# Attention with mixed heads: seven high parts move to ScalarE, and each part of v is split two slots ahead of its products

## The chip, the cores and the metric

The kernel runs on one core of one Trainium2 chip. The metric is device time in microseconds (us) of one execution. In this text TensorE is PE in the rows, VectorE is DVE, ScalarE is ACT, GpSimd is POOL, and SyncE, whose queue issues most DMAs, is SP.

## The reference

Four batches, twelve heads, 448 positions, 64 columns a head. Scores of all heads are mixed with `w_pre` ahead of the softmax and with `w_post` behind it; two gated layers follow.

```python
scores = scale * np.matmul(q, k.transpose(0, 1, 3, 2))
scores = np.einsum('bhij,hg->bgij', scores, w_pre)
scores = scores - np.max(scores, axis=-1, keepdims=True)
attn = np.exp(scores)
attn = attn / (np.sum(attn, axis=-1, keepdims=True) + 1e-09)
attn = np.einsum('bhij,hg->bgij', attn, w_post)
out = np.matmul(attn, v)
...
h = (x @ w1) * (x @ w2) @ w3
x = h @ w_out
out = np.maximum(x @ w_in, 0.0) ** 2 @ w_out2
```

## The kernel before

Products that need more than 16 bits are made of two parts: a high part (rounded) and a low part (what is left), and three products of parts.

The 448 rows of a batch are cut into four pieces of 110, 110, 110 and 118 rows (`SUP`, numbered s = 0 to 15; piece 4b is the first of batch b), and each piece into blocks of ten rows (`BLK`, numbered u = 0 to 179, the last of a batch of eight rows). A main loop goes over slots, one per block, and writes out by hand the order of all engines. In slot u stand, among others:

- the DMA of block u + 5 from the scores (`regroup`, `Bt<-S`, L279), at the slot's end, on SP's queue;
- in odd slots, the mixing product of blocks u + 1 and u + 2 (`premix`, L285, TensorE), which reads `Bt`; one premix is two matmul records, so a pair is four;
- the negated row maximum (`negmax`, L299, VectorE) and the exponential (`expo`, L307, ScalarE) of block u;
- of block u - 2 the high part `EH` (`split_h`), made by GpSimd (L354), or, for odd blocks from `LAST_EH` = 166 on, by ScalarE (L352); of odd blocks GpSimd makes the low part too (L365, L366), of even blocks VectorE makes it one slot later (L368);
- the second mixing product of block u - 4 (`postmix`, L381, TensorE) and the eviction of block u - 5 in two parts, `ATh` by ScalarE (L397) and `ATl` by VectorE (L403). The product has two PSUM buffers, so a postmix waits for `ATl` of two blocks earlier;
- what a table of events adds: `qk` (scores of a later piece) and `av` (products with v of an earlier piece, L495) at the end of a slot; `split_k`, `split_kl` (L197, GpSimd), `split_q`, `split_ql` (L227), `split_v` (the high part `Vh`, L467, ScalarE) and `split_vl` (the low part `Vl`, L474, VectorE), the last four behind the slot's other work; the evictions of `av` (`put_xh`, `put_xl`, L523) and their stores (`store_x`, L531, SP).

Each batch's v comes in six parts (two heads each), and piece 4b needs them first. Its two raw buffers (`vraw`) are used again for the first two chunks of the later layers' weights, which SP's queue loads in slots 153 and 156:

```python
v_last = first[NSUP - 4]
W_LOADS = (v_last + 18, v_last + 21)
...
        if u in W_LOADS:
            load_to(W_LOADS.index(u) + 1)
```

`first[s]` is the first block of piece s; `v_last` is 135. These loads stand at the start of their slots. A load into a buffer waits for the last reader of what was in it, and SP's queue issues in order. k of batch b is split in six steps, one in every second slot: blocks 26 to 36 for batch 1, 70 to 80 for batch 2, 116 to 126 for batch 3.

Of the kernel before, what the change touches and what calls it, by code (L numbers as in the profile page):

```python
# [35 lines left out]
def talking_heads_attention_moe_moe2(  # L36
# [28 lines left out]
    SUP = []  # L65
# [199 lines left out]
    NB = len(BLK)  # L265
# [73 lines left out]
    def inverse(u):  # L339
        return nsum[u][: BLK[u][2] * H, 5, u % 2 : u % 2 + 1]  # L340

    def seven(x):
        return x.rearrange("p (a b) -> p a b", a=EG)

    def low_on_pool(u):
        return u % 2 == 1

    def split_h(u):
        n = BLK[u][2] * H
        EH[u] = bp.tile([NBK, S], F16, tag="EH", name="EH", bufs=4)  # L350
        if low_on_pool(u) and u >= LAST_EH:
            nc.scalar.activation(seven(EH[u][:n]), Ex[u][:n], AF.Copy, scale=inverse(u))  # L352
            return
        nc.gpsimd.tensor_scalar(  # L354
            seven(EH[u][:n]), Ex[u][:n], inverse(u), 1.0, op0=ALU.mult, op1=ALU.mult
        )
# [47 lines left out]
            ATs[s][1][:, :, :, a], src, ATs[s][0][:, :, :, a], op=ALU.subtract  # L404
        )

    LAST_EH = NB - 14

    def v_raw():
        return bp.tile([P, 6 * NCH, D], F32, tag="vraw", name="vraw", bufs=2)  # L410
# [129 lines left out]
    first = {}  # L540
# [7 lines left out]
    LOAD, FIRST, MID, LOW, END = range(5)  # L548

    def at(slot, kind, f, *a):  # L550
        events.setdefault(slot, []).append((kind, len(events), f, a))

    low_k = set()
    for s in range(2, NSUP):
        b = SUP[s][0]
        base = first[s - 1]
        L = first[s] - base
        qs = [base - 4 + p * L // NDC for p in range(NDC)]
        for p in range(NDC):
            at(qs[p], END, qk, s, p)  # L560
            at(qs[p] + 1, FIRST, evict_s, s, p)
            if p % 3 == 0:
                at(qs[p] - 9, LOAD, load_q, s, p // 3)
                at(qs[p] - 5, MID, split_q, s, p // 3, None)
                at(qs[p] - 4 + (p == 0 and qs[p] - 4 in low_k), LOW, split_ql, s, p // 3)
        if s % 4 == 0:
            ks = [(first[s - 2] + 4) // 2 * 2 + 2 * p for p in range(NDC)]
            for p in range(NDC):
                assert ks[p] + 1 < qs[p]
                at(ks[p], MID, split_k, b, p, None)  # L570
                at(ks[p] + 1, LOW, split_kl, b, p)
                low_k.add(ks[p] + 1)
                at(ks[p] - 4, LOAD, load_k, b, p)
    for b in range(B):
        f = first[4 * b]
        for i, slot in ((0, 9), (2, 11), (4, 13)):
            at(f + slot, MID, scale_v, b, i)
        for hg in range(2):
            for i in range(3):
                if b or hg:  # L580
                    at(f - 4 + 3 * hg + i if b else i + 1, LOAD, load_v, b, hg, i)
                at(f + 3 * hg + i + 1, MID, sum_v, b, hg, i)
                at(f + 3 * hg + i + 13, MID, split_v, b, hg, i)
                at(f + 3 * hg + i + 14, LOW, split_vl, b, hg, i)
    qk_at = sorted(x for x in events if any(e[2] is qk for e in events[x]))
    for s in range(NSUP - 1):
        for p in range(NDC):
            lo = first[s + 1] + LAG + 1
            at_qk = [x for x in qk_at if lo <= x < lo + SUP[s + 1][3]]
            slot = at_qk[p] if len(at_qk) == NDC else lo + (0, 1, 3, 4, 6, 7)[p]  # L590
            for part in range(2):
                at(slot, END, av, s, p, part)
            if p % 3 == 2:
                at(slot + 1, FIRST, put_xh, s, p // 3)
                at(slot + 1, MID, put_xl, s, p // 3)
                if s < NSUP - 2:
                    at(slot + 2, END, store_x, s, p // 3)
# [511 lines left out]
    for u in range(NB + LAG + 2):  # L1109
# [38 lines left out]
        if 0 <= u - 2 < NB:  # L1148
            split_h(u - 2)
            if low_on_pool(u - 2):  # L1150
                split_l(u - 2)
# [459 lines left out]
```

## Time and profile before

| what | value |
|---|---|
| time, median of 3 runs | 1283.51 us (1282.63 to 1283.73) |
| the profiled execution: its time, its span | 1283.09 us, 1281.4 us |
| TensorE, busy share of the span | 98% |
| VectorE, ScalarE, GpSimd, busy share | 76%, 55%, 34% |
| attention part (180 slots) | about the first 440 us |

The span runs from the first to the last instruction; the time has 1.7 us around it. Once the start is over, a pair of slots takes between 4.1 and 6.0 us (from one `expo` of an even slot to the next).

### The profile page before, as it was taken

What the parts mean: (1) busy time and instruction counts of PE and PEld (TensorE: products, weight loads), DVE (VectorE), ACT (ScalarE), POOL (GpSimd) and SP (SyncE); (2) the same over time, 40 slices, a digit from 0 to 9 for tenths busy, and PEclk for the clock granted to TensorE, in tenths of its full rate; (3) what the DMA queues carried; (4) which work ended last, traced back from release to release, by engine and by line L of the source; (5) the groups of instructions that cost most, each with busy time, mean ns of one, the idle gap of its engine ahead of it and who ended that gap; (6) DMA issues with size and microseconds to landing.
All of it is one profiled execution on the core that took longest, in us unless ns stands there. A gap on an engine that the chain in (4) does not pass through costs nothing. (4 is left out here: it accounts for less than half of the span.)

```text
span 1281.4 us, 25951 instructions
## 1 busy us (share of the span) xinstructions
PE 1258.4 (98%) x10192; PEld 775.3 (61%) x10192; DVE 980.1 (76%) x2032; ACT 704.1 (55%) x1367; POOL 430.9 (34%) x502
## 2 busy tenths in 40 slices
PE   7999999999999999999999999999999999999998
PEld 3666766766766655555569855555555555555555
DVE  6988897898899868876849766437568779797776
ACT  6877876877887635443424444336844353534520
POOL 3898799789878401110003200000000000001000
PEclk9999999999999999999999999999999999999999
DMA  6466455555656734354223234004141322324004
GB/s 192 122 163 166 119 149 145 151 134 139 167 147 168 212 76 110 101 109 129 91 83 132 82 79 81 9 3 87 38 107 35 90 78 38 78 49 105 5 10 173
DMA packets 82174, 132.92 MB, mean 104 GB/s; under 512 B 30820, under 2 KB 67812, under 8 KB 82052
## 3 DMA queue, kind: packets, MB, share of 16 engines
q1 hardware_dynamic: 75924, 123.45, 35.6%
q0 software_dynamic: 2992, 5.42, 3.0%
q10 hardware_dynamic: 3136, 2.40, 0.7%
q8 instruction: 80, 1.31, 0.4%
q14 instruction: 42, 0.34, 0.1%
HBM read 80.78 MB, written 11.92 MB: 72 GB/s over the span
## 5 line engine op out<-in xcount | busy, mean ns | idle before, releaser
L1046 PE MATMUL mm<-x,w 128*128 128x448 f16 x2196 | 416.7, 352 | 0.0
L1046 PEld LDWEIGHTS <-w 128*128 128x128 f16 x2304 | 224.9, 98 | 209.2
L1488 PE MATMUL mm<-w,g 128*128 128x384 f16 x1344 | 219.7, 326 | 0.0
L1488 PEld LDWEIGHTS <-g 128*128 128x128 f16 x1344 | 131.5, 98 | 87.4 <-issue 0.2
L285 PE MATMUL p<-Bt,wpre_k 120*120 120x448 f32 x360 | 158.9, 560 | 5.0 <-DMA Bt<-S 3.3
L381 PEld LDWEIGHTS <-EH 120*112 120x112 f16 (+1 forms) x1440 | 125.0, 130 | 50.9 <-issue 41.6
L354 POOL TENSOR_SCALAR EH<-E,st 120x448 f16<-120x448 f32 x173 | 127.9, 749 | 46.3 <-DVE st L337 32.2
L403 DVE TENSOR_TENSOR ATl<-o,ATh 112x480 f16<-112x480 f32 x180 | 116.2, 645 | 31.9 <-ACT ATh L397 31.7
L397 ACT CAST ATh<-o 112x480 f16<-112x480 f32 x180 | 100.9, 561 | 58.5 <-PE o L381 53.7
L381 PE MATMUL o<-wph,EH 120*112 120x120 f16 x720 | 124.1, 219 | 7.7 <-DVE ATl L403 6.4
L307 ACT ACTIVATE E<-p,st 120x448 f32<-120x448 f32 x180 | 115.7, 643 | 21.9 <-DVE st L299 12.3
L1497 DVE SCALAR_TENSOR_TENSOR acc<-mm,sv,acc 128x384 f32<-128x384 f32 x196 | 112.1, 609 | 14.2 <-PE mm L1488 13.5
L381 PE MATMUL o<-wph,EL 120*112 120x120 f16 x720 | 122.2, 216 | 0.0
L381 PE MATMUL o<-wpl,EH 120*112 120x120 f16 x720 | 122.2, 216 | 0.0
L805 POOL DMA_DIRECT2D across<-tot x23 | 12.8, 556 | 316.7 <-ACT xa L791 316.7
L299 DVE TENSOR_REDUCE st<-p 120x1 f32<-120x448 f32 x180 | 110.1, 612 | 1.7 <-PE p L285 1.5
L1046 PE MATMUL mm<-h,M 128*128 128x448 f16 x576 | 109.8, 353 | 0.7 <-ACT M L1218 0.5
L366 POOL TENSOR_TENSOR EL<-F,EH 120x448 f16<-120x448 f32 (+1 forms) x90 | 100.6, 1118 | 23.8 <-issue 16.0
L791 ACT ACTIVATE xa<-xa 128x768 f32<-128x768 f32 x54 | 45.5, 842 | 93.4 <-DVE xa L787 75.4
L381 PEld LDWEIGHTS <-EL 120*112 120x112 f16 x720 | 93.6, 130 | 0.0
L368 DVE SCALAR_TENSOR_TENSOR EL<-E,st,EH 120x448 f16<-120x448 f32 (+1 forms) x90 | 82.5, 917 | 12.7 <-POOL EH L354 11.8
L1046 PEld LDWEIGHTS <-M 128*128 128x128 f16 x576 | 55.9, 98 | 53.9 <-DVE M L1214 1.9
(217 smaller groups left out, 2057.9 us busy)
## 6 DMA issues: line engine op xcount, KB each, us to landing
Bt<-S SPq DMA_DIRECT2D x176, 210.0 KB
raw<-in_moe_w_out_dram SPq DMA_DIRECT2D x24, 768.0 KB
raw<-in_moe_w_in_dram SPq DMA_DIRECT2D x16, 768.0 KB
raw<-in_moe_w_dram SPq DMA_DIRECT2D x14, 768.0 KB
raw<-in_moe_w_dram SPq DMA_DIRECT2D x16, 512.0 KB
vraw<-in_v_dram SPq DMA_DIRECT2D x24, 224.0 KB
out_dram<-acc SPq DMA_DIRECT2D x28, 192.0 KB
kraw<-in_k_dram SPq DMA_DIRECT2D x22, 224.0 KB
```

Of the source, the lines that this page charges most:

```text
L285: nc.tensor.matmul(pt[: n * H, :S], wpre_k.rearrange("p t g -> p (t g)")[: n * H, : n * H], Bt.pop(u)[: n * H], start=True, stop=True,)
L299: nc.vector.tensor_reduce(nsum[u][:n, 0, j : j + 1], Pp[u][:n, :S], axis=AX.X, op=ALU.max, negate=True)
L307: nc.scalar.activation(e[:n], Pp.pop(u)[:n, :S].rearrange("p (a b) -> p a b", a=EG), AF.Exp, bias=t[:n, 0, j : j + 1], scale=1.0, accum_ou ...
L354: nc.gpsimd.tensor_scalar(seven(EH[u][:n]), Ex[u][:n], inverse(u), 1.0, op0=ALU.mult, op1=ALU.mult)
L366: nc.gpsimd.tensor_tensor(a, f, b, op=ALU.subtract)
L368: nc.vector.scalar_tensor_tensor(a, e, inverse(u), b, op0=ALU.mult, op1=ALU.subtract)
L381: nc.tensor.matmul(pt[:CP, c * n : (c + 1) * n], a[:n, c * CP : (c + 1) * CP], w[:n, :n], start=(i == 0), stop=(i == 2),)
L397: nc.scalar.copy(ATs[s][0][:, :, :, m * NR : m * NR + nr], src)
L403: nc.vector.tensor_tensor(ATs[s][1][:, :, :, a], src, ATs[s][0][:, :, :, a], op=ALU.subtract)
L1046: nc.tensor.matmul(pt[:, :S], w[a][:, cs], x[z][:, sl], start=(c == 0 and i == 0), stop=(c == len(parts) - 1 and i == 2),)
L1488: nc.tensor.matmul(pt[:, :OH], gs[j][a][:, ts_], ws[j][0][:, w, os_], start=(n == 0), stop=(n == 5),)
L1497: nc.vector.scalar_tensor_tensor(d, pt[:, :OH], sv[:, v : v + 1], d, op0=ALU.mult, op1=ALU.add)
```

## The change

The high part of an odd block is made by ScalarE also for the blocks in `full`. That set is filled where the first step of a batch's scores stands in an even slot, which holds for piece 8 (batch 2) alone: blocks 70 to 83, so seven odd blocks, 71 to 83. And each part of v is split at fixed distances from its own first product: `split_v` two slots ahead of `av` of piece 4b and `split_vl` one slot ahead, where before the six parts were split in six slots running, 13 to 18 slots into the batch (`split_vl` 14 to 19).

```diff
-        if low_on_pool(u) and u >= LAST_EH:
+        if low_on_pool(u) and (u in full or u >= LAST_EH):
             nc.scalar.activation(seven(EH[u][:n]), Ex[u][:n], AF.Copy, scale=inverse(u))
             return
...
-    LAST_EH = NB - 14
+    LAST_EH, full = NB - 14, set()
...
             ks = [(first[s - 2] + 4) // 2 * 2 + 2 * p for p in range(NDC)]
+            if qs[0] % 2 == 0:
+                full.update(range(ks[0], ks[-1] + 4))
...
                 at(f + 3 * hg + i + 1, MID, sum_v, b, hg, i)
-                at(f + 3 * hg + i + 13, MID, split_v, b, hg, i)
-                at(f + 3 * hg + i + 14, LOW, split_vl, b, hg, i)
...
             slot = at_qk[p] if len(at_qk) == NDC else lo + (0, 1, 3, 4, 6, 7)[p]
+            if s % 4 == 0:
+                b = SUP[s][0]
+                assert slot - 2 > first[s] + 13
+                at(slot - 2, MID, split_v, b, *divmod(p, 3))
+                at(slot - 1, LOW, split_vl, b, *divmod(p, 3))
```

For batch 3 the six low parts stood in slots 149 to 154; they stand now in slots 150, 152, 153, 155, 157 and 159. The weight loads of slots 153 and 156 stay where they were.

GpSimd's queue where k of batch 2 is split (`EH`, `F` and `EL` are the parts of a block, `kl` and `ql` low parts of k and q), a piece of the difference:

```order
-L354 TENSOR_SCALAR EH<-E,st 120x448 x2
-L365 TENSOR_SCALAR F<-E,st 120x7x64
-L366 TENSOR_TENSOR EL<-F,EH 120x448
-L197 TENSOR_TENSOR kl<-kraw,kh 128x448
...
+L354 TENSOR_SCALAR EH<-E,st 120x448
+L365 TENSOR_SCALAR F<-E,st 120x7x64
+L366 TENSOR_TENSOR EL<-F,EH 120x448
+L197 TENSOR_TENSOR kl<-kraw,kh 128x448
```

One of the two `EH` of each pair of slots is gone from there, seven in all.

VectorE's queue around the last low part of v of batch 3, before:

```order
L299 TENSOR_REDUCE st<-p 120x1
L323 TENSOR_SCALAR st<-st 120x6
L337 RECIPROCAL st<-st 120x2
L403 TENSOR_TENSOR ATl<-o,ATh 112x48x10
L474 SCALAR_TENSOR_TENSOR Vl<-vraw,vs,Vh 112x512
```

and of the change (L785 and L789 are the first steps of decoding the first weight chunk):

```order
L403 TENSOR_TENSOR ATl<-o,ATh 112x48x10
L785 TENSOR_SCALAR Vh<-vraw 128x768
L789 TENSOR_SCALAR kraw<-kraw 128x768
L299 TENSOR_REDUCE st<-p 120x1
L368 SCALAR_TENSOR_TENSOR EL<-E,st,EH 120x448
L403 TENSOR_TENSOR ATl<-o,ATh 112x48x10
L474 SCALAR_TENSOR_TENSOR Vl<-vraw,vs,Vh 112x512
```

The last low part moved from slot 154 to the end of slot 159, behind `ATl` of block 154.

SP's queue around the two weight loads (`vraw<-in_moe_w_dram`), with what each DMA waits for, before:

```order
L729 DMA vraw<-in_moe_w_dram 128x1536 [waits DMAHW1_49,DVE_49]
L279 DMA Bt<-S 120x1x448 [waits DMAHW2_49,PE_49]
L279 DMA Bt<-S 120x1x448 [waits DMAHW3_49,PE_49]
L279 DMA Bt<-S 120x1x448 [waits DMAHW4_49,PE_49]
L729 DMA vraw<-in_moe_w_dram 128x1536 [waits DMAHW5_49,DVE_49,Activation_49]
L531 DMA x_d<-xt 128x3x110 [waits DMAHW6_49,Activation_49]
L531 DMA x_d<-xt 128x3x110 [waits DMAHW7_49,DVE_49]
L279 DMA Bt<-S 120x1x448 [waits DMAHW0_49,PE_49]
```

and of the change, where the load's line is L734:

```order
L734 DMA vraw<-in_moe_w_dram 128x1536 [waits DMAHW1_49,DVE_49,Activation_49]
L279 DMA Bt<-S 120x1x448 [waits DMAHW2_49,PE_49]
L279 DMA Bt<-S 120x1x448 [waits DMAHW3_49,PE_49]
L279 DMA Bt<-S 120x1x448 [waits DMAHW4_49,PE_49]
L734 DMA vraw<-in_moe_w_dram 128x1536 [waits DMAHW5_49,DVE_49,Activation_49]
L531 DMA x_d<-xt 128x3x110 [waits DMAHW6_49]
L531 DMA x_d<-xt 128x3x110 [waits DMAHW7_49]
L279 DMA Bt<-S 120x1x448 [waits DMAHW0_49,PE_49]
```

No DMA changed its place. Behind the second load the two stores no longer wait for ScalarE and VectorE themselves: the load ahead of them waits for later instructions of both, the last `Vh` of batch 3 (slot 158) and the last `Vl` (slot 159). The first load waits for the `Vl` of slot 153. The `Bt` right behind the stores is that of block 161, whose premix stands in slot 159; the three ahead of the second load are blocks 158 to 160.

## Rows read from the trace of the kernel before

**Rows 1.** the page's first part: busy us and share of each engine

```profile
PE 1258.4 (98%) x10192; PEld 775.3 (61%) x10192; DVE 980.1 (76%) x2032; ACT 704.1 (55%) x1367; POOL 430.9 (34%) x502
```

**Rows 2.** busy us by engine, six slot pairs, k of batches 1, 2 split

```profile
80.48:108.33 27.85, 27.02 (x352) 18.75 (x351) 23.55 (x50) 20.09 (x45) 27.35 (x31) 1.00 0.57 146
187.13:217.16 30.03, 27.34 (x351) 19.10 (x348) 24.47 (x50) 19.81 (x45) 29.53 (x33) 1.00 0.49 121
```

**Rows 3.** waits of PE, 187-217, 48-56, 258-272 us: total us, times, longest

```profile
PE o L381 <- DVE ATl L403: 2.7, 4, 0.9
...
PE o L381 <- DVE ATl L403: 1.0, 1, 1.0
...
PE o L381 <- DVE ATl L403: 1.1, 2, 0.8
```

**Rows 4.** waits of DVE, 185 to 215 us

```profile
DVE EL L368 <- POOL EH L354: 4.7, 4, 1.4
```

**Rows 5.** one line's instructions, POOL's high part and ACT's: ns least/median/most

```profile
L354 POOL TENSOR_SCALAR EH<-E,st x173: 632/642/1850, 22.7 to 435.6; 120x448 f16<-120x448 f32 x170, 96x448 f16<-96x448 f32 x3
...
L352 ACT ACTIVATE EH<-E,st x7: 655/657/689, 411.2 to 441.7; 120x448 f16<-120x448 f32 x6, 96x448 f16<-96x448 f32 x1
```

**Rows 6.** VectorE's low part of v, all 24: ns least/median/most

```profile
L474 DVE SCALAR_TENSOR_TENSOR Vl<-vraw,vs,Vh x24: 733/905/1393, 48.7 to 378.6; 112x512 f16<-112x512 f32 x24
```

**Rows 7.** timeline of DVE: start us, us, line, tiles

```profile
263.54 0.51 DVE L523 SCALAR_TENSOR_TENSOR xt<-a,xt 128x354 f16<-128x354 f32 x1
```

**Rows 8.** timeline of PE, first product with Vl

```profile
265.31 0.21 PE L495 MATMUL a<-ATh,Vl 112*64 112x110 f16 x2
```

**Rows 9.** timeline of SP: when DMAs were issued

```profile
373.71 0.45 SPq L729 DMA_DIRECT2D vraw<-in_moe_w_dram  x1
...
379.53 0.47 SPq L729 DMA_DIRECT2D vraw<-in_moe_w_dram  x1
380.30 1.82 SPq L531 DMA_DIRECT2D x_d<-xt  x2
382.21 9.40 SPq L279 DMA_DIRECT2D Bt<-S  x6
```

**Rows 10.** timeline of DVE: low parts of v, and ATl of block 154

```profile
376.00 0.33 DVE L219 CAST qh<-qraw 128x354 fp32r<-128x354 f32 x1
...
378.56 0.90 DVE L474 SCALAR_TENSOR_TENSOR Vl<-vraw,vs,Vh 112x512 f16<-112x512 f32 x1
...
389.25 0.65 DVE L403 TENSOR_TENSOR ATl<-o,ATh 112x480 f16<-112x480 f32 x1
```

**Rows 11.** timeline of PE: premix of blocks 158, 159 and 160, 161

```profile
383.59 1.76 PE L285 MATMUL p<-Bt,wpre_k 120*120 120x448 f32 x4
...
388.05 1.76 PE L285 MATMUL p<-Bt,wpre_k 120*120 120x448 f32 x4
```

**Rows 12.** DMAs by kind: count, KB each

```profile
Bt<-S SPq DMA_DIRECT2D x176, 210.0 KB
...
x_d<-xt SPq DMA_DIRECT2D x44, 82.5 KB
...
vraw<-in_moe_w_dram SPq DMA_DIRECT2D x2, 768.0 KB
```

**Rows 13.** windows, last columns the granted clock, DMA share, GB/s

```profile
380.00:388.00 8.00, 8.00 (x115) 5.83 (x113) 7.33 (x16) 6.85 (x16) 7.83 (x10) 1.00 0.82 239
384.00:385.00 1.00, 1.00 (x4) 0.50 (x3) 1.00 (x2) 1.00 (x4) 1.00 (x2) 1.00 0.87 287
```

**Rows 14.** windows at the end of the span

```profile
1280.00:1281.00 1.00, 0.00 (x0) 0.00 (x0) 0.00 (x0) 0.00 (x0) 0.00 (x0) 0.85 0.00 0
```

**Rows 15.** timeline of PE at the end of the span

```profile
1273.69 3.90 PE L1488 MATMUL mm<-w,g 128*128 128x384 f16 x23
```

**Rows 16.** timeline of PE: the first filler products, and later ones

```profile
1.26 3.29 PE L622 MATMUL a<-ATl 128*128 128x512 f16 x8 [1.26 <-DVE ATl L617]
...
22.48 1.03 PE L622 MATMUL a<-ATl 128*128 128x512 f16 x4
```

## The prediction

> **What bounds the kernel now.** I read the page first: TensorE is busy for 1258.4 of 1281.4 us [rows 1], so the kernel is as long as TensorE's queue, and a change outside TensorE can only give or take the waits in it, 23.0 us in all. Then I asked for TensorE's waits in the stretches that the change touches. Where k of batch 2 is split it waits four times, 2.7 us, and in the two stretches where v of batches 0 and 2 is split once and twice, 1.0 and 1.1 us; each time a postmix needs a PSUM buffer that VectorE's `ATl` has not yet emptied [rows 3]. VectorE's own waits then say what is late ahead of that `ATl`. In the stretch of k it is GpSimd's `EH`, four times, 4.7 us [rows 4]. The windows agree: six slot pairs with the same products (352 and 351 records) take 27.85 us in batch 1 and 30.03 us in batch 2, and GpSimd is busy for 29.53 of the latter [rows 2]. Last I read SP's timeline around the two weight loads, since the order shows that their waits change.
>
> **The change, part by part.**
>
> *The seven high parts.* GpSimd loses 7 x 0.642 = 4.5 us and ScalarE gains 7 x 0.657 = 4.6 us [rows 5]. ScalarE is busy for 19.81 of the 30.03 us [rows 2], so it has 10.2 us free and takes them. GpSimd then has some 25.0 us of work in a stretch that is 27.85 us long where nothing is late, so `EH` is no longer what VectorE waits for. The gain lies between 2.2 us (30.03 less 27.85, as in batch 1, which has waits of its own) and 2.7 us (all four waits). If ScalarE were late instead it is nothing. I take 2.5.
>
> *v split later.* Where TensorE waits today, VectorE has just made low parts of v ahead of the `ATl` that is late. One costs 0.73 to 1.39 us, 0.905 in the middle [rows 6]. With the change the first of them stands behind that `ATl`, and the six are spread over ten slots instead of six. So the waits of 1.0 and 1.1 us should go; the bounds are nothing and 2.1 us, and I take 2.1, because the low parts taken away ahead of the `ATl` are as long as the waits. A new wait comes in: TensorE's first product with `Vl` now follows the low part closely. At the tightest of the 24 places VectorE is done with the instruction ahead at 264.05 us [rows 7] and the product starts at 265.31 us [rows 8], 1.26 us later. A low part of 0.905 us fits, one of 1.39 us is 0.13 us late; I take nothing, and 0.4 us (three times that) as the bound.
>
> *SP's second weight load.* Not one DMA moves, but the load of slot 156 must wait until the buffer's old content, the second half of v of batch 3, has been read, and the last reader moved to the end of slot 159. In the run before that reader ends at 378.56 + 0.90 = 379.46 us [rows 10] and the load is issued at 379.53 us [rows 9], so SP already waits for it, and everything behind stands with it. The Trainium skill says the same of any DMA: a semaphore wait happens on the issuing sequencer, the DMA engines only consume their queues ("DMA: Bandwidth & Descriptors", section "Anatomy of one DMA"); the 0.07 us between these two rows agrees, and it is the rule that speaks against this change.
>
> In the new order the reader follows `ATl` of block 154, which ends at 389.25 + 0.65 = 389.90 us [rows 10]. VectorE has by then done five low parts of the batch, as against six before, so it comes there no later. The low part ends at 390.8 us and the load is issued 11.3 us later than before. Behind it wait two stores, which nobody needs soon, and the `Bt` of blocks 161 to 164. TensorE wants block 161 in slot 159: the premixes of blocks 160 and 161 start at 388.05 us and take 1.76 us, so the second starts at 388.9 us [rows 11]. That product is held, and with TensorE's queue in order so are the postmix, `av` and all that ScalarE and VectorE would do next.
>
> How long? The load is issued in 0.47 us [rows 9], so nothing flows before 391.3 us. Then 768 + 2 x 82.5 + 210 = 1143 KB [rows 12], 1.17 MB, have to pass. In the eight busy microseconds of the run before the rate is 239 GB/s [rows 13]: 4.9 us. With 0.9 us for start and landing (my choice) block 161 is there at 397.1 us: 8.2 us of waiting. The low bound takes the best microsecond, 287 GB/s [rows 13], and no start: 4.1 us, 395.4 us, 6.5 us of waiting. The high bound is what the run before allows: there the load was issued at 379.53 us and block 161 was in place by 388.9 us, so it needed at most 9.4 us; 390.8 + 9.4 = 400.2 us, 11.3 us of waiting. I take 8.2, nearer the low end, because in the run before the stores waited too and older blocks were still in transfer. By the fit for one DMA of the Trainium skill's page "DMA: Bandwidth & Descriptors" (2.0 us plus the bytes at 436 GB/s, same section; measured on another kind of queue) the 1.17 MB would take 4.7 us, the wait would be 6.6 us and the sum 1286.6 us, an estimate.
>
> *SP's first weight load.* It now waits for the low part of slot 153, which follows the cast that ends at 376.33 us [rows 10]: 377.2 us, 3.5 us later than its 373.71 us [rows 9]. By the same reckoning (978 KB, 4.2 us) block 158 is there at 377.2 + 0.5 + 4.2 + 0.9 = 382.8 us, and TensorE wants it at 383.59 us [rows 11]. So nothing is lost, but it is near: the bound is 3.5 us, if block 158 landed just in time before. I take 0.3.
>
> *TensorE's clock.* The longest wait of rows 3 is 1.0 us; one of 8 us is new. At the end of the span the last product ends at 1273.69 + 3.90 = 1277.59 us [rows 15], and the granted clock of 1280 to 1281 us is 0.85 [rows 14], which is 1.0 (2.4 GHz) for the first 0.7 us and 0.5 (1.2 GHz) after it: it fell 3.1 us after TensorE stopped. The start shows what it takes to come back: eight filler products need 3.29 us, four later ones 1.03 us [rows 16]; the eight lost 3.29 - 2.06 = 1.2 us. I add 1.2 us, between nothing (the clock holds) and 3.3 us (all of such a stretch). The Trainium skill's rule is that the slow clock is the default state and activity lifts it ("TensorE: Matmul & The Clock Gate", "Part 1: The HAM clock gate"); rows 14 to 16 agree, and it too speaks against this change.
>
> *Sum.* Gains 2.5 + 2.1 = 4.6 us; losses 8.2 + 0.3 + 1.2 = 9.7 us; together 5.1 us longer. The attention part's delay reaches the end in full, because what follows is TensorE's queue and no later wait is that long. Against the profiled execution's 1283.09 us (0.42 us under the median, so no correction is needed): 1288.2 us.
>
> **Rivals.** *The load is not in the way* (faster). If the last `Vl` were done by 382.6 us (388.9 less the 6.3 us from issue to landing), block 161 would be in time. For it: VectorE has room where low parts were taken away. Against it: the `ATl` ahead of it reads a product of slot 158, and slot 159 starts at 388 us. Only the gains are left: 1283.1 - 4.6 = 1278.5 us. Chance 0.07.
>
> *A short wait* (about the same). The transfer runs at its best rate and the clock holds: 1283.1 - 4.6 + 6.5 = 1285.0 us. For it: the queues are empty when the load comes, unlike before. Chance 0.16.
>
> *The gains don't come* (the change doesn't do what it says). ScalarE makes `EH` ahead of the next `ATh`, so the `ATl` that GpSimd made late would be late by ScalarE, and the spread low parts, 0.9 us in slots where VectorE is busy for 23.55 of 27.85 us [rows 2], would hold back as much as before. Against it: ScalarE has 10.2 us free for 4.6. 1283.1 + 9.7 = 1292.8 us. Chance 0.10.
>
> **How the numbers follow.** My forecast, 1288.2 us, has 0.67. It and the last rival are slower by over 0.2% (2.6 us, about what a measurement of this kernel can tell): 0.77. The short wait is within 0.2%: 0.16. Faster: 0.07. The range reaches down to the short wait with somewhat more gain (4.6 + 2.5 us), 1282.5 us, and up to the high bound of the wait with 2.2 us for the clock and the first load: 1283.1 - 4.6 + 11.3 + 2.2 = 1292.0, and 1293.0 us to take in the last rival; what is left out is the first rival and the far ends. The forecast's own range is 1286 to 1292 us.
>
> **What would show it.** In the changed kernel TensorE should have one wait of 6.5 to 11.3 us in a premix, released by the DMA of `Bt`, near 385 to 395 us; SP's second weight load should be issued right after the last `Vl`, and VectorE's last `Vl` should follow the first steps of decoding. A granted clock under 1 just behind that wait shows the clock's term. The four waits of rows 3 near 200 us and those near 52, 264 and 269 us should be gone, and VectorE should no longer wait for GpSimd's `EH` there. No wait at `Bt` makes the forecast wrong by its largest term; waits of postmix near 200 us make it wrong by the gains.

## The result, and the profile after

The changed kernel takes 1292.27 us (median of 6 runs, 1290.23 to 1294.23) against 1283.68 us: 1.0065 times the time before, 95% interval 1.0052 to 1.0078. Its profiled execution took 1292.72 us, 9.63 more than the one of before. The forecast was 1288.2 us, with 1286 to 1292 us as its own range. The direction and the mechanism of the largest term were right; the time lies 0.3 us above that range, and a loss of 3.8 us was not foreseen.

The page of the changed kernel, its first line and two groups of TensorE (busy us, mean ns, then the idle time ahead of them and its releaser); the first answers to [rows 1]:

```profile
PE 1261.1 (98%) x10192; PEld 776.3 (60%) x10192; DVE 979.3 (76%) x2032; ACT 709.4 (55%) x1374; POOL 429.5 (33%) x495
...
L285 PE MATMUL p<-Bt,wpre_k 120*120 120x448 f32 x360 | 160.8, 563 | 14.6 <-DMA Bt<-S 13.7
...
L381 PE MATMUL o<-wph,EH 120*112 120x120 f16 x720 | 124.7, 219 | 5.2 <-DVE ATl L403 3.9
```

ScalarE has seven instructions more and GpSimd seven fewer, as the diff says. TensorE has 29.9 us without work in place of 23.0. Where they lie, and what else grew, is told by the lengths of stretches, worked out from the starts of the exponential (L307) of the blocks at their ends, in the profiled executions:

| blocks | what changed there | before | after | change | predicted |
|---|---|---|---|---|---|
| 0 to 10 | nothing | 19.61 | 20.13 | +0.5 | 0 |
| 10 to 24, 100 to 114 | v of batches 0, 2 split later | 31.78, 34.22 | 30.53, 32.96 | -2.5 | -2.1 |
| 24 to 40, 114 to 130 | the last low part of v stands at their start; k of batches 1, 3 is split | 36.76, 36.76 | 38.66, 38.64 | **+3.8** | 0 |
| 54 to 70, 144 to 156 | v of batches 1, 3 split later | 36.70, 28.13 | 36.31, 27.68 | -0.8 | 0 |
| 70 to 86 | seven high parts on ScalarE | 38.94 | 36.42 | -2.5 | -2.5 |
| 156 to 166 | SP's second weight load | 21.72 | 32.99 | **+11.3** | +9.7 |
| 166 to the end | | 877.28 | 877.30 | 0 | 0 |

A block stands for its slot; the stretches not listed change by 0.1 us in all. First the largest. TensorE's waits of the changed kernel from 380 to 402 us (us in total, times, longest), and SP's queue there:

```profile
PE p L285 <- DMA Bt<-S: 8.3, 2, 8.0
```

```profile
375.35 0.35 SPq L734 DMA_DIRECT2D vraw<-in_moe_w_dram  x1
...
389.47 0.35 SPq L734 DMA_DIRECT2D vraw<-in_moe_w_dram  x1
389.88 0.95 SPq L531 DMA_DIRECT2D x_d<-xt  x2
390.93 1.69 SPq L279 DMA_DIRECT2D Bt<-S  x2
```

VectorE's and TensorE's timelines give what is on either side of it:

```profile
388.66 0.75 DVE L474 SCALAR_TENSOR_TENSOR Vl<-vraw,vs,Vh 112x512 f16<-112x512 f32 x1
```

```profile
386.89 1.01 PE L285 MATMUL p<-Bt,wpre_k 120*120 120x448 f32 x2
...
395.87 1.82 PE L285 MATMUL p<-Bt,wpre_k 120*120 120x448 f32 x2 [7.96 <-DMA Bt<-S]
```

The last low part ends at 389.41 us, the load is issued 0.06 us later, the `Bt` of block 161 stands behind it and the two stores, and TensorE, out of work at 387.90 us, starts again at 395.87 us. That premix of two records takes 1.82 us where the one ahead took 1.01. The windows say why (the number ahead of the last two is the granted clock):

```profile
388.00:390.00 2.00, 0.00 (x0) 0.00 (x0) 2.00 (x5) 0.55 (x2) 1.92 (x2) 1.00 0.00 0
390.00:392.00 2.00, 0.00 (x0) 0.00 (x0) 0.17 (x2) 0.00 (x0) 0.92 (x2) 0.80 0.73 178
...
396.00:398.00 2.00, 2.00 (x8) 1.05 (x9) 0.00 (x0) 0.00 (x0) 0.00 (x0) 0.50 0.56 133
...
400.00:402.00 2.00, 2.00 (x31) 1.37 (x30) 2.00 (x4) 1.14 (x4) 1.92 (x2) 0.64 0.35 97
402.00:404.00 2.00, 2.00 (x18) 1.10 (x13) 1.89 (x6) 2.00 (x5) 1.04 (x1) 1.00 0.11 26
```

The clock falls from 1.00 (2.4 GHz) to 0.50 (1.2 GHz) while TensorE stands, about 391.2 us, and comes back near 401.4 us. So the 11.3 us are 7.96 of waiting at the second load, 0.30 at the first, and 3.0 us more, nearly all of it slow work: 5.6 us at half the speed cost 2.8 us.

Then the loss that was not predicted. TensorE's waits of the changed kernel from 86 to 108 us, where k of batch 1 is split, and where the run before waits 0.2 us for `ATl` and never for `Bt`:

```profile
PE o L381 <- DVE ATl L403: 1.3, 3, 0.7
PE p L285 <- DMA Bt<-S: 0.7, 1, 0.7
```

With a shorter wait for `E` these make 1.3 us more of waiting than before in blocks 24 to 40. The other 0.6 us of the 1.9 appears as busy time of TensorE (36.55 us in place of 35.92), whose ends are modelled.

The gains are plain. From 185 to 219 us TensorE waits once, 0.5 us, in place of four times [rows 3], and VectorE's wait for `EH` from 185 to 215 us went from 4.7 us [rows 4] to 1.8. The waits near 52, 264 and 269 us are gone.

```profile
PE o L381 <- DVE ATl L403: 0.5, 1, 0.5
```

```profile
DVE EL L368 <- POOL EH L354: 1.8, 2, 1.1
```

**Where the k split got slower.** The first two low parts of k of batch 1, with the casts of k and q (`kh`, L191; `qh`, L219) near them, on GpSimd and VectorE, before:

```profile
78.96 1.15 POOL L197 TENSOR_TENSOR kl<-kraw,kh 128x448 fp32r<-128x448 f32 x1
83.58 1.15 POOL L197 TENSOR_TENSOR kl<-kraw,kh 128x448 fp32r<-128x448 f32 x1
...
80.04 0.38 DVE L191 CAST kh<-kraw 128x448 fp32r<-128x448 f32 x1
84.50 0.41 DVE L219 CAST qh<-qraw 128x330 fp32r<-128x330 f32 x1
84.83 0.38 DVE L191 CAST kh<-kraw 128x448 fp32r<-128x448 f32 x1
```

and in the changed kernel:

```profile
79.26 1.65 POOL L197 TENSOR_TENSOR kl<-kraw,kh 128x448 fp32r<-128x448 f32 x1
84.19 1.88 POOL L197 TENSOR_TENSOR kl<-kraw,kh 128x448 fp32r<-128x448 f32 x1
...
79.53 0.38 DVE L191 CAST kh<-kraw 128x448 fp32r<-128x448 f32 x1
84.45 0.32 DVE L219 CAST qh<-qraw 128x330 fp32r<-128x330 f32 x1
84.69 0.39 DVE L191 CAST kh<-kraw 128x448 fp32r<-128x448 f32 x1
```

Before, the next cast starts where the low part ends (80.04 against 78.96 + 1.15 = 80.11 us), or 0.23 us ahead of that (84.50 against 84.73 us). After, it starts 0.27 us into it, and GpSimd's instruction is 0.50 us longer; with two casts inside, 0.73 us. Two of the six low parts of k were as long before (1.65 and 1.89 us); now four are, and two of the three of q. All nine take 13.0 us in place of 10.9: 2.1 us more, in a stretch that is 1.9 us longer. VectorE stands and waits for GpSimd meanwhile; from 70 to 108 us, before and after:

```profile
DVE EL L368 <- POOL EH L354: 2.2, 2, 1.1
```

```profile
DVE EL L368 <- POOL EH L354: 6.5, 6, 1.5
```

Which instruction meets which is a matter of VectorE's place against GpSimd's, and two low parts of v now stand right ahead, in blocks 22 and 24. That became the theory to test.

### The profile page after: what moved, and what is told of

Same layout as the page of the kernel before. It is cut to its first block, busy times and chain, and to the rows that moved or that the text cites. A ratio compares the mean times of both kernels' runs of the same rounds, so it can differ in the third digit from the quotient of the medians.

```text
span 1291.0 us, 25949 instructions
## 1 busy us (share of the span) xinstructions
PE 1261.1 (98%) x10192; PEld 776.3 (60%) x10192; DVE 979.3 (76%) x2032; ACT 709.4 (55%) x1374; POOL 429.5 (33%) x495
## 5 line engine op out<-in xcount | busy, mean ns | idle before, releaser
L403 DVE TENSOR_TENSOR ATl<-o,ATh 112x480 f16<-112x480 f32 x180 | 116.1, 645 | 35.9 <-ACT ATh L397 35.6
L354 POOL TENSOR_SCALAR EH<-E,st 120x448 f16<-120x448 f32 x166 | 123.2, 751 | 53.4 <-DVE st L337 31.9
L307 ACT ACTIVATE E<-p,st 120x448 f32<-120x448 f32 x180 | 115.9, 644 | 26.6 <-DVE st L299 19.6
L285 PEld LDWEIGHTS p<-Bt,wpre_k 120*120 120x120 f32 x360 | 57.0, 183 | 59.6 <-issue 27.0
```

Of the source, the lines that this page charges most:

```text
L285: nc.tensor.matmul(pt[: n * H, :S], wpre_k.rearrange("p t g -> p (t g)")[: n * H, : n * H], Bt.pop(u)[: n * H], start=True, stop=True,)
L307: nc.scalar.activation(e[:n], Pp.pop(u)[:n, :S].rearrange("p (a b) -> p a b", a=EG), AF.Exp, bias=t[:n, 0, j : j + 1], scale=1.0, accum_ou ...
L354: nc.gpsimd.tensor_scalar(seven(EH[u][:n]), Ex[u][:n], inverse(u), 1.0, op0=ALU.mult, op1=ALU.mult)
L403: nc.vector.tensor_tensor(ATs[s][1][:, :, :, a], src, ATs[s][0][:, :, :, a], op=ALU.subtract)
```

## The experiments

All ratios are to the kernel before, with 95% intervals; before itself had a median of 1283.5 to 1283.9 us beside them.

**1. The high parts alone** (the first three hunks of the diff without the move of v).

> The kernel before with ScalarE's seven high parts alone; v is split where it was. Theory (the gain is GpSimd's, and stands by itself): blocks 70 to 86 take 36.4 us in place of 38.9, nothing else moves, and the time is 2.5 us under the kernel before, 1281.2. Rival (the gain comes only together with the later splits of v, or the earlier TensorE runs into a wait right behind): under 1 us, 1283. Blocks 24 to 40, where the changed kernel lost 1.9 us, take 36.75 us as before under the theory that the splits of v make that loss; 38 or more if ScalarE's high parts make it.

Measured: 1280.66 us, 0.9975 [0.9964, 0.9985]. Blocks 70 to 86 take 36.40 us, 24 to 40 take 36.75 and 114 to 130 36.74. The first theory holds: 2.5 us, by itself, and the loss in the k splits is not its doing.

**2. The weight loads behind their readers.**

```diff
-    W_LOADS = (v_last + 18, v_last + 21)
+    W_LOADS = (v_last + 19, v_last + 25)
```

> The changed kernel with both weight loads issued behind the last reader of the buffer that they take (in blocks 154 and 160 in place of 153 and 156). Theory (SP stands at the second load, and the clock falls because TensorE stands still for it): the waits of 7.96 and 0.30 us go, the clock stays at 1.00 there, blocks 156 to 166 take 21.7 us in place of 33.0, and the time is 1281.0 us, 11.3 under the changed kernel. Rival (a load in block 160 finds a wait of its own, the decode of the second chunk or the Bt that share the queue with it): 2 us or more of that stay, 1283 to 1285. Rival (the clock falls for another reason): 2.7 us stay, 1283.7, with a granted clock of 0.50 to 0.64 in some stretch behind block 156.

Measured: 1281.64 us, 0.9983 [0.9974, 0.9992]. Blocks 156 to 166 take 22.24 us; no window there is below 1.00, and from 376 to 402 us TensorE has one wait:

```profile
PE o L381 <- DVE ATl L403: 0.3, 1, 0.3
```

So 10.8 of the 11.3 us were the loads' place in SP's queue with what followed from it, the clock's fall too; in these blocks nothing else in the change makes the clock fall.

**3. The load of the fifth part of k one block later** (`p` counts from 0, so `p == 4` is the fifth of six loads; the text below calls it the third).

```diff
-                at(ks[p] - 4, LOAD, load_k, b, p)
+                at(ks[p] - 4 + (p == 4), LOAD, load_k, b, p)
```

> The changed kernel with the third load of k issued one block later in each batch, behind the low part of k that it waits for. Theory A (SP's queue stands at this load, and the Bt behind it are late): the premix waits of 0.67 and 0.97 us in the k splits of batches 1 and 3 go, and 1.6 us or more of the 3.8 lost there come back: 1288.5 to 1290.7. Theory B (the queue is a sign only; GpSimd is late, and TensorE would wait for EL and ATl a little further on): the premix waits go, but waits of postmix for ATl grow by as much, and the time stays at 1292.

Measured: 1291.28 us, 1.0057 [1.0042, 1.0072]. From 86 to 110 us:

```profile
PE o L381 <- DVE ATl L403: 1.9, 3, 0.9
PE p L285 <- ACT E L307: 0.2, 1, 0.2
```

The wait for `Bt` is gone, and the waits for `ATl` grew from 1.3 to 1.9 us; blocks 24 to 40 still take 38.62 us. Theory B: the queue only shows the lateness first. The median is 1 us lower than the changed kernel's, with intervals that overlap; the k splits do not explain it. Its profile is shorter in blocks 156 to 166 (31.14 us in place of 32.99): TensorE's wait at the second load ends at 395.85 us, as in the changed kernel, but the clock comes back sooner, at 399.0 us:

```profile
398.00:400.00 2.00, 2.00 (x25) 1.91 (x25) 0.50 (x1) 1.09 (x4) 1.06 (x2) 0.76 0.59 147
```

So 3.1 us of work were slow here and 5.6 in the changed kernel. In experiments 4 to 7, which keep this load, it is 5.6, 3.8, 3.2 and 4.0 us, behind waits of 7.7 to 8.2 us. At half the speed that costs 1.6 to 2.8 us, and it differs from profile to profile.

**4. The last parts of v earlier in batches 0 and 2.**

```diff
-                at(slot - 2, MID, split_v, b, *divmod(p, 3))
-                at(slot - 1, LOW, split_vl, b, *divmod(p, 3))
+                x = slot - 2 - (0, 0, 0, 1, 2, 3)[p] * (b % 2 == 0)
+                at(x, MID, split_v, b, *divmod(p, 3))
+                at(x + 1, LOW, split_vl, b, *divmod(p, 3))
```

> The changed kernel with the last three parts of v of batches 0 and 2 split one, two and three blocks earlier (the low parts stand up to block 21 and not up to 24, and four blocks lie between them and the k split of the next batch). Theory (the late low parts, on VectorE right ahead of the k split, make GpSimd late in it): blocks 24 to 40 and 114 to 130 take 36.8 us each again in place of 38.7, less than 1.5 us of the gain in blocks 10 to 24 and 100 to 114 is lost, and the time is 1288.5 to 1290. Rival (the loss comes from TensorE being earlier by the gain made just before, and any gain there is given back in the k split): the sum of the stretch 10 to 40 does not change, and the time stays at 1292.

Measured: 1288.23 us, 1.0034 [1.0023, 1.0046]. Blocks 24 to 40 and 114 to 130 take 36.74 and 36.76 us again, and blocks 10 to 24 and 100 to 114 30.90 and 32.76 (before 31.78 and 34.22). Nearly all of the gain stays and all of the loss goes: it was the late low parts, and not TensorE's being earlier. They are not enough by themselves, though. Low parts of batch 1 stand in blocks 67 and 69 of the changed kernel, right ahead of the split of k of batch 2, and blocks 70 to 86 take 36.42 us, as in experiment 1 (36.40), where v is unmoved; there ScalarE makes seven of the high parts.

**5. More work on VectorE in those places** (on top of 4; one run). In blocks 22 and 24 a second low part of v whose result is not used, in blocks 112 to 114 a second row maximum:

```diff
+        if b == 0:
+            at(f + 22, LOW, more_low, b)
+            at(f + 24, LOW, more_low, b)
...
+        if u in (112, 113, 114):
+            more_max(u)
```

> The kernel with the earlier tail, and more work on VectorE ahead of two k splits: in blocks 22 and 24 one more instruction each like a low part of v (1.03 us, from SBUF to SBUF, its result is not used); in blocks 112, 113 and 114 the maximum of the block's logits once more (0.61 us each, read from PSUM). Theory (GpSimd's instructions get longer while VectorE works in SBUF): blocks 24 to 40 go from 36.7 to 38 or more, with kl at 1.7 us in place of 1.2; blocks 114 to 130 stay under 37.2. Rival (VectorE's own lateness makes the loss, whatever it reads): both stretches get longer alike, by 1 us or more. Rival (the lateness of v's parts for their products mattered, not VectorE's load): neither changes.

Measured: 1294.49 us. Blocks 24 to 40 take 39.88 us, 114 to 130 38.96. The six low parts of k of batch 1 from 70 to 112 us in experiment 4 (ns least/median/most):

```profile
L197 POOL TENSOR_TENSOR kl<-kraw,kh x6: 1133/1220/1888, 77.6 to 102.3; 128x448 fp32r<-128x448 f32 x6
```

and here, of batches 1 and 3:

```profile
L197 POOL TENSOR_TENSOR kl<-kraw,kh x6: 1124/1648/1894, 81.2 to 107.0; 128x448 fp32r<-128x448 f32 x6
...
L197 POOL TENSOR_TENSOR kl<-kraw,kh x6: 1132/1644/1894, 293.1 to 319.0; 128x448 fp32r<-128x448 f32 x6
```

My theory failed in one point: what the added work reads does not matter. Either kind makes VectorE late ahead of the split, and either then has GpSimd's low parts long. VectorE's lateness is the trigger, the casts inside `kl` are what becomes of it. Against experiment 4, blocks 10 to 40 and 100 to 130 are 3.1 us longer each, and the nine low parts of k and q 2.1 us; what the other 1.0 us comes from is open.

**6. The casts of k on ScalarE** (in the changed kernel, batches 1 and 3).

```diff
-                at(ks[p], MID, split_k, b, p, None)
+                at(ks[p], MID, split_k, b, p, None, nc.scalar if b % 2 else None)
```

> The changed kernel with the high parts of k (kh, the casts of 0.385 us) made by ScalarE in place of VectorE for batches 1 and 3; the late low parts of v stay where the change put them. Theory (the low parts of v shift VectorE so that its casts of k and q start inside GpSimd's low parts of k and q, and GpSimd stands still meanwhile: kl goes from 1.15 to 1.65 us with one cast inside, to 1.88 with two, ql from 0.89 to 1.40): kl is 1.15 us beside no cast of k, at most 1.4 with one of q, ql 0.9, and blocks 24 to 40 and 114 to 130 drop from 38.7 to 36.8 or less, so 1292.3 - 3.8 = 1288.5 or less. Rival (VectorE's 2 us of added work make the loss by themselves, whatever GpSimd does): ScalarE takes 2.3 us of casts off VectorE too, but kl stays long. Rival (ScalarE becomes late with S and E): the stretches stay at 38 or more with premix waiting for E.

Measured: 1288.55 us, 1.0038 [1.0023, 1.0053]. Blocks 24 to 40 and 114 to 130 take 36.75 us each, though v's low parts stay late:

```profile
L197 POOL TENSOR_TENSOR kl<-kraw,kh x6: 1127/1137/1596, 80.5 to 103.9; 128x448 fp32r<-128x448 f32 x6
```

The only long one (1.60 us) has a cast of q 0.27 us into it. Another cast of q starts 0.7 us into a low part of k, at 85.55 us: there the low part stays at 1.14 us, and the cast takes 0.65 us in place of 0.32. ScalarE was not late by it beyond the one premix wait of 0.85 us for `E` in each stretch (0.7 before).

**7. The casts on VectorE in a longer form** (in the changed kernel, batches 1 and 3; one run).

```diff
+        elif b % 2:
+            nc.vector.scalar_tensor_tensor(hh, t, 1.0, t, op0=ALU.mult, op1=ALU.max)
```

> The changed kernel with the casts of k of batches 1 and 3 still on VectorE, as an operation with two inputs (the larger of k and k), some 0.9 us each in place of 0.385 by the low parts of v (1.03 us for 512 columns). Theory (GpSimd stands still only beside the short one-input cast): kl is 1.15 to 1.4 us though a cast lies beside it, and the two stretches change by what VectorE's 3 us more cost, from 38.7 to between 37 and 39. Rival (any work of VectorE from SBUF to SBUF holds GpSimd up for as long as it takes): kl of 2.0 us and more, both stretches 41 or more.

Measured: 1294.10 us; both stretches 40.03 us. One such cast, and the `kl` that it starts 0.27 us into:

```profile
79.98 0.61 DVE L191 SCALAR_TENSOR_TENSOR kh<-kraw 128x448 fp32r<-128x448 f32 x1
```

```profile
79.71 1.88 POOL L199 TENSOR_TENSOR kl<-kraw,kh 128x448 fp32r<-128x448 f32 x1
```

The operation took 0.61 us and not 0.9, and `kl` is 0.73 us longer: for 0.385 us it was 0.50. So the theory's limit to the short one-input cast is wrong. In both forms GpSimd's record ends 1.0 us after VectorE's operation does (here 81.59 and 80.59 us). The nine low parts of a stretch take 14.4 us, 3.5 more than before, and the stretch is 3.3 us longer.

**8. The three repairs together** (1, 2 and 4).

> ScalarE's seven high parts, the splits of v with the earlier tail in batches 0 and 2, and the weight loads of blocks 154 and 160, together. If the three causes found so far are all there is, the terms add: the kernel with the earlier tail, 1288.2, less what the later weight loads took off blocks 156 to 166 (33.0 to 22.2, against 32.7 here: 10.4) gives 1277.8, 6 us under the kernel before. Rival (an earlier TensorE runs into the next wait, so that part of the sum is given back): 1280 or more.

Measured: 1278.44 us, 0.9956 [0.9941, 0.9971], against a sum of 1277.8. No new wait eats the terms; it is the fastest kernel here, 5.2 us under the one before. From 86 to 110 us TensorE waits

```profile
PE p L285 <- ACT E L307: 0.6, 1, 0.6
PE o L381 <- DVE ATl L403: 0.2, 1, 0.2
```

**9. The same with ScalarE's high parts in all three k splits** (the condition on `qs[0]` left out).

> The same with ScalarE's high parts in all three k splits (27 of them or so in place of 7 or 8). Theory (GpSimd is what the k split waits for): blocks 24 to 40 and 114 to 130 drop from 36.7 to about 36.4, the length of blocks 70 to 86 now, and the time is 0.6 us lower than the three together, 1277.2. Rival (ScalarE, which evicts S there, makes expo late, and the premix waits for E): those stretches get longer, 1278.5 or more.

Measured: 1280.56 us, 0.9974 [0.9964, 0.9984]. Blocks 24 to 40 take 37.61 us, 114 to 130 37.59, and from 86 to 110 us TensorE waits

```profile
PE p L285 <- ACT E L307: 0.9, 1, 0.9
PE p L285 <- DMA Bt<-S: 0.4, 1, 0.4
```

This fits the rival, that ScalarE becomes late: VectorE waits 2.8 us for its `ATh` from 70 to 109 us, 1.2 in experiment 8. What helps in blocks 70 to 86 harms in the two other splits.

**10. The three with the casts of k on ScalarE.**

> The three together (1278.4) with the high parts of k of batches 1 and 3 made by ScalarE. Theory: two kl of each batch and one ql that were long there already (1.65 and 1.88 us) get short, 1.2 to 1.7 us less of GpSimd in a stretch that GpSimd sets, and TensorE gets up to 0.6 us of its 0.8 us of waits there back in each: 1277.2 to 1278. Rival (ScalarE is too full, as with the high parts of E): 1279 or more.

Measured: 1278.81 us, 0.9962 [0.9948, 0.9976], no different from 8. The windows of blocks 24 to 40 in 8 and here (TensorE, its loads, VectorE, ScalarE, GpSimd):

```profile
70.68:107.42 36.74, 35.91 (x467) 25.02 (x466) 31.59 (x68) 26.92 (x60) 36.07 (x41) 1.00 0.57 146
```

```profile
70.83:107.57 36.74, 35.89 (x468) 24.94 (x467) 29.71 (x63) 29.22 (x67) 36.07 (x42) 1.00 0.58 150
```

The low parts of k are 1.0 us shorter in all and the stretch is not: TensorE has 35.9 us of work in it, and where it no longer waits for `ATl` (0.2 us in 8) it waits longer for `E` (0.9 us in place of 0.6). GpSimd's spans fill 36.07 us in both, so that sum does not tell whether GpSimd is late.

**11 and 12. The second weight load two blocks and one block later** (158 and 157, in the changed kernel), so that TensorE has more work in hand.

> The changed kernel with its second weight load two blocks later, in block 158, still ahead of the low part that it waits for (block 159). SP stands there as before, but the first Bt behind it belongs to block 163 and not 161, so TensorE has 4.4 us more of work in hand: a wait of 7.96 - 4.4 = 3.6 us in place of 7.96. Theory A (the clock falls only after a stop of more than some 3 us, so most of its loss goes too): granted clock 1.00 or a dip under 2 us, 1281 + 3.6 to 4.6, so 1285 to 1286. Theory B (any stop of a few us brings the full dip of 5.5 us at half the clock): 1281 + 3.6 + 2.7 = 1287.5.

Measured: 1288.16 us (1285.29 to 1288.81), 1.0030 [1.0019, 1.0041]; the profiled execution 1286.15. Its wait is 2.93 us, and the window behind it is at 1.00, but the clock falls later, behind a second wait of 1.5 us near 415 us:

```profile
PE p L285 <- DMA Bt<-S: 2.9, 1, 2.9
```

```profile
396.00:400.00 4.00, 4.00 (x54) 2.76 (x52) 2.97 (x5) 3.17 (x7) 3.40 (x3) 1.00 0.57 131
...
416.00:420.00 4.00, 3.88 (x17) 2.23 (x18) 3.09 (x7) 1.35 (x4) 1.38 (x2) 0.64 0.75 216
```

> The changed kernel with its second weight load one block later, in block 157, so that TensorE has 2.2 us more of work in hand than in the changed kernel: a wait of 7.96 - 2.2 = 5.8, or 5.1 by the 2.93 us that the load in block 158 left. Theory A (the clock falls some 3 us after TensorE stops and needs about 5.5 us of work to come back, whatever the wait beyond that): the dip behind the wait is as long as in the changed kernel, 2.7 us lost, and blocks 156 to 166 take 22.2 + 5.1 + 2.7 = 30.0 us. Theory B (the low clock lasts some 10 us from its fall, wait included): about 8 us of work at half the clock, 4 us lost, 31.3 us. Theory C (a wait of this length is short enough, as 2.9 us was): 1.00 throughout, 27.3 us.

Measured: 1289.05 us, 1.0037 [1.0023, 1.0052]. Two waits, 3.50 and 0.95 us; blocks 156 to 166 take 29.26 us:

```profile
PE p L285 <- DMA Bt<-S: 4.5, 2, 3.5
```

```profile
392.00:394.00 2.00, 0.00 (x0) 0.00 (x0) 2.00 (x3) 1.65 (x5) 1.92 (x3) 1.00 0.79 263
...
396.00:398.00 2.00, 1.47 (x2) 0.69 (x3) 0.47 (x3) 0.00 (x0) 0.64 (x1) 0.50 0.55 130
...
402.00:404.00 2.00, 2.00 (x29) 1.40 (x28) 1.44 (x4) 1.53 (x3) 1.62 (x2) 0.91 0.20 47
```

Less the 22.24 us of experiment 2 and the 4.45 us of waiting, 2.6 us went to the clock. The same reckoning for the changed kernel (32.99 less 22.24 and 8.26) leaves 2.5, so waits half as long cost as much slow work here. Theory A's figure fits this profile and not those of experiments 3, 5, 6 and 7, where 3.1 to 4.0 us of work were slow behind longer waits; theory B's loss of 4 us fits none. What sets the length stays open. The wait of 2.93 us (experiment 11) fits neither theory of its own text: its profile shows the clock falling later, the median is 2 us above the profiled execution, and what the runs without a profile did there stays open.

## Why the prediction was right, and where it was wrong

*The seven high parts*: 2.5 us predicted, 2.5 measured, and additive (experiment 1).

*v split later*: right for batches 0 and 2 as far as it went, 2.5 us in place of 2.1, which was also the bound, and 0.8 us more in batches 1 and 3, which the sum left out.

*The first products with the low parts*: none was late, as taken.

*SP's second weight load*: the mechanism was right in each of its steps, the size partly by luck. The low part ended at 389.41 us in place of 390.8, and TensorE stopped 1.0 us sooner than reckoned, so two errors nearly cancelled; from issue to restart 6.4 us were measured for 6.3. 8.0 us in place of 8.2, and 0.30 for the first load in place of 0.3. Experiment 2 shows the cause.

*TensorE's clock*: the term was mis-sized, 1.2 us in place of 3.0. I took the loss of the eight filler products at the start as what it takes to come back; behind this stop 5.6 us of work ran at half the clock, and in other profiles with the same stop 3.1 to 5.6 us. The measured 3.0 us is inside the bound of 3.3.

*The step that failed* is the cost of v's later low parts. The prediction asked only who reads them and whether VectorE has room for six of 0.9 us; it did not ask what VectorE and GpSimd do next in blocks 24 to 40 and 114 to 130, where the diff moves nothing but the low part at their start. Two low parts in blocks 22 and 24 make VectorE late as the k split begins, more of its casts then start early inside GpSimd's low parts of k and q, and TensorE waits for what is late behind them: 3.8 us. That the low parts in these places are the trigger is shown by taking them away (4) and by putting other work there (5). That the casts inside `kl` lengthen it is shown by 6 and 7. That GpSimd's longer instructions carry the loss to TensorE is borne out by their size: the nine low parts take 0, 2.1 and 3.5 us more than before in experiment 4, the changed kernel and experiment 7, the stretch 0, 1.9 and 3.3 us; and VectorE waits for GpSimd there. That VectorE's own 2 us add nothing is not shown: experiment 6 takes both away at once.

The sum: 5.1 predicted, plus 3.8 for the k splits and 1.8 for the clock, less 1.3 of further gain, plus 0.5 at the start, less 0.3 in the rest (the load's 0.2 and the stretches not listed) is 9.6. The rival "The gains don't come" names almost the time measured (1292.8 us) and is wrong: the gains came, and nearly as much was lost elsewhere. The measured time is inside the stated range only by the last microsecond, from 1292.0 to 1293.0 us, which was added for this rival; that is luck. "The load is not in the way" fell with the wait of 7.96 us, "a short wait" with its length and the clock.

## What to carry to other kernels

When a buffer's last reader is moved to a later place, move the transfer that fills the buffer next behind it as well: in an in-order queue it holds up everything behind it, and a stop of TensorE can be paid a second time at half the clock, as here behind waits of 3.5 us and more. When an instruction is moved, look not only at who reads it but at what now follows closely on its engine, and which instructions of VectorE then run beside GpSimd's, also in stretches that the diff doesn't touch. A change that nets a loss can hold two gains: taken apart, it gave 5.2 us.

## What the runs showed of the hardware

GpSimd's subtraction of 128x448 (two inputs in SBUF) takes 1.12 to 1.15 us with no cast of VectorE inside, 1.65 with one of 0.385 us that starts 0.27 us into it, 1.88 with two or with one operation of 0.61 us. A row maximum from PSUM inside it adds nothing: in experiment 6 one of 1.14 us has all of the 0.61 us of one inside. A cast that starts later is held up itself. In the changed kernel, where k of batch 2 is split:

```profile
197.38 1.15 POOL L197 TENSOR_TENSOR kl<-kraw,kh 128x448 fp32r<-128x448 f32 x1
```

```profile
198.02 0.77 DVE L191 CAST kh<-kraw 128x448 fp32r<-128x448 f32 x1
```

The cast starts 0.64 us into the low part and takes 0.77 us in place of 0.385; GpSimd's instruction takes 1.15 us all the same. The 14 profiles have 185 low parts of k with a cast of VectorE inside (in experiment 7 the longer form), and they fall into two kinds. Where the first cast starts ahead of the record or up to 0.54 us into it, GpSimd's record ends 1.0 us after the last cast's (the latest start: experiment 1 at 200.80 us, 1.91 us long). Where it starts from 0.57 us on, the low part takes 1.13 to 1.16 us and the cast ends 0.2 to 0.3 us after it (the earliest: the kernel before at 187.27 us, with a cast of 0.84 us). The Trainium skill says that VectorE and GpSimd share a pair of SBUF ports and that the one that starts first keeps it for its whole instruction ("SBUF — State Buffer", section "Who interferes with whom"). The sharing agrees, and so does the waiting of one for the other; but the start of a record does not tell who is first, since a cast that came up to 0.54 us after GpSimd's start went ahead of it. If GpSimd's turn begins some 0.55 us into the record of this instruction, an estimate from these two starts, the rule fits all 185.

The profiles differ at the start, too. TensorE waits 1.5 to 2.2 us for a `Bt` near 30 us in each of the 14 profiles. In four of them (experiments 3, 5, 6 and 9; waits of 1.8 to 2.0 us) the clock then falls, and blocks 0 to 10 take 21.3 to 21.5 us in place of 19.1 to 20.2; in the others (1.5 to 2.2 us) it holds, so the length of the wait alone does not decide. From 28 to 40 us, experiments 4 and 6:

```profile
28.00:40.00 12.00, 10.71 (x100) 7.08 (x100) 9.38 (x22) 8.58 (x22) 8.83 (x12) 1.00 0.60 161
```

```profile
28.00:40.00 12.00, 9.80 (x71) 6.62 (x71) 8.58 (x19) 7.69 (x19) 8.42 (x12) 0.86 0.59 155
```

That is some 1.7 us, as much as an edit here is worth, and no edit made it.
